# Program order and engine choice of the first feed-forward tiles rearranged in a fused linear-attention and feed-forward kernel

## The chip, the cores and the metric

The kernel runs on one core of a Trainium2 chip. The core has five engines with a queue each: TensorE (PE in the profile, its weight loads shown as PEld), VectorE (DVE), ScalarE (ACT), GpSimd (POOL) and SyncE (SP), which here issues every load and store. The metric is the device time of one execution in microseconds (us), taken as the median of several.

## The reference

For four batches and four heads, with 1088 positions of 32 numbers each, queries, keys and values go through a feature map: each vector x gives a = S1 x and b = S2 x (eight numbers each) and the 64 products a_i b_j. The output of the attention is

```
kv  = sum over positions of k_p[f] * v[d]        (64 x 32 for each batch and head)
z   = sum over positions of k_p[f]
num = q_p @ kv ;  den = q_p @ z + 1e-6 ;  x = num / den
```

The 4352 rows of x, 128 numbers wide (four heads of 32), then pass a feed-forward network with 2048 hidden units:

```
h = x @ w_in ;  r = max(h, 0) ;  g = s * r * r + b ;  out = g @ w_out
```

S1, S2, w_in and w_out arrive as 64-bit floats and are turned into 32-bit ones on the chip.

## The kernel before, in words

**Tiles.** The 4352 rows are cut into nine feed-forward tiles, number 0 with 256 rows and numbers 1 to 8 with 512. A tile has eight units (jp = 0 to 7), each 256 of the 2048 hidden units. A unit is a generator, `ffn(t, jp)`, named by two digits ("03" is tile 0, unit 3). Its steps are: the product into `hp` (PE, L571), the relu (L131 or L133), the square (L140 or L142), and the product into `ops` (PE, L571). In tile 0 the products use 32-bit operands directly, four matmul records for each product (two blocks of 128 hidden units, two records each). In tiles 1 to 8 each operand is split into a high and a low part of a faster type, `xh` and `xl`, `uh` and `ul`, `wih` and `wil`, `woh` and `wol`, and a product has six matmuls; `split_u` (L121 and L565) makes `uh` and `ul`.

**Weights.** w0 to w9 are ten weight blocks: even numbers are parts of w_in, odd ones of w_out; w0 to w3 have 256 columns, w4 to w9 have 512. `load_weights` (L185, steps "Lw0" to "Lw9") issues loads of 256 KB, one for a small block and two for a large one. `split_weights` (steps "w0" to "w9") turns a block into floats in three steps: a Prelu on ACT (L202, the "prelude" below), an integer scaling called bits (L127 on ACT or L125 on DVE), and a join on DVE (L193); then come the high part (L121) and the low part (L136). Raw blocks of w_in share four buffers, and so do those of w_out, so the fifth raw block of a kind waits on SP until the join of the first has read its buffer. The fifth of w_in is w4 in both orders; the loads of w_in before it are w0, w2, w8, w6 before the change and w2, w0, w8, w6 after it.

**Attention.** `first_keys` ("k0") makes the key features of batch 0 in three groups (PE L295, copies L121, outer products on DVE L136), `first_key_sums` ("e0", ended by `masked`, `spread` and `key_sums`) and `first_value_sums` ("v0", PE L253, 72 records) sum them; the constants and the values of batch 0 arrive in one load of 662 KB, `vc_sb` (L158). `kvphase` ("k1" to "k3") does the other batches. `direct_features` makes the query features of tiles 0 and 1 on the engines ("q0", "q1": PE L402, copies `br` L121, products `pq` on DVE L410), `stored_features` those of the others by way of DRAM ("q2" to "q8": PE L419, copy `abq`, stores L428, loads L435 and L439, a product). `first_denominators` ("d0"), `first_numerators` ("n0") and `attend` ("n1" to "n8") multiply features and sums (PE L464) and divide; n0 ends with `x` for tile 0 (DVE L495), and the first unit can start behind it.

**Order.** Nothing is scheduled by a machine at run time. `ORDER` is a list of steps; each token advances the generator of that name by one step, and each engine runs its instructions in the order in which the steps issued them. "Lk0" and its like are loads on SP's one queue, in order: a load that waits holds up all behind it. `ON_DVE` names the steps that run on DVE; those that are not named run on ACT (copies, relus, squares, bits) or on POOL (pairwise products). "c" and "z" are warming products of 256 and 512 columns (L650) whose result is never read. PSUM has two `hp` buffers, one `ops` and three `psa`.

```
for c in ORDER.split():
    next(gens[c], None)
```

The first ten loads before the change, in SP's order, are: the S matrices (80 KB), keys and queries of batch 0 (192 and 512 KB), w0, w2 (256 KB each), vc_sb (662 KB), the queries of tile 1, w8, w6 and w1 (256 KB each), 2,982 KB together. Then come w4, w6 (its second part), the queries of tile 2, w4 (second part), w3, w5, w5, w7, w7, w8 and the keys of batch 1. The first steps are the same work in the same place in both orders on PE: keys, q0, key sums, value sums, q1, turned sums, d0, n1, n0, q2 and then the units 00, 01, 03.

Of the kernel before, what the change touches and what calls it, by code (L numbers as in the profile page):

```python
# [38 lines left out]
DIRECT = (0, 1)  # L39
FIRST_F32 = (0, 1, 2, 3, 4, 5, 6, 7)  # L40
ORDER = """
c z Ls c z Lk0 c Lk0 Lw0 Lw2 s Lv0 Lq1 Lw8 z s c z c s s z z s w0 w2 k0 s c k0 Lw6 k0 k0 k0 Lw1 k0 k0 w0 k0 w0 Lw4
Lw6 q0 c q0 Lq2 k0 Lw4 q0 Lw3 Lw5 Lw5 Lw7 Lw7 e0 e0 q0 Lw8 Lk1 e0 v0 v0 q0 w2 Lk1 e0 v0 w2 v0 q1 q1 q1 q1 e0 e0 w1
v0 z w1 q1 d0 v0 n1 d0 n0 w6 w6 q2 d0 c w4 d0 d0 n0 n1 Lv1 w4 w4 w1 q2 w4 w3 00 00 00 01 w3 w0 03 01 01 w5 w6 q2 00
02 Lw9 03 w8 w3 n1 w3 n1 01 03 Lw9 02 w5 04 02 w7 q2 w5 w7 n1 Lk3 q2 w0 03 05 n1 05 Lk3 02 w8 Lq3 w1 05 Lq4 q1 n1 04
q2 n1 k1 w8 06 w6 w7 04 n1 w9 05 07 06 w3 04 k1 w4 06 k1 n1 w9 w9 k1 w9 07 13 k1 07 w1 Lv1 Lv3 w6 06 q2 w5 13 13 10
q2 07 q2 k1 k3 10 q3 10 q3 13 14 10 07 w2 q2 13 k1 k3 k1 12 w2 w5 14 q3 k1 10 15 w7 q2 07 12 Lv2 14 12 k1 q3 Lk2 k3
10 k3 12 Lv3 11 14 w8 k3 12 w7 n2 k3 15 12 14 w8 07 q3 w9 15 n2 n2 13 14 11 15 11 17 n2 n2 Lk2 15 n2 16 15 q3 q3 n2
n2 11 11 Lq6 17 q4 q3 k2 16 n2 n2 20 k3 16 11 16 17 q3 q4 25 16 q4 17 q3 k3 q4 q4 16 20 22 20 k2 17 17 25 25 20 25
17 20 22 17 24 20 q4 22 q3 k2 22 25 24 24 k3 q4 Lv2 23 22 n3 q4 Lq5 23 24 q6 n3 23 q6 22 n3 Lq8 n3 24 21 23 21 27 q6  # L50
21 n3 k2 q4 25 23 q6 21 n3 27 26 24 n3 23 k2 27 n3 21 k2 q6 27 q8 q6 n3 q6 q6 n3 26 q4 26 k2 21 q0 30 q8 q4 k2 k2 27
q6 26 33 q6 k3 30 k2 30 q8 26 q5 n4 q5 q8 33 32 n4 30 30 26 33 n4 27 n4 n4 33 n4 33 32 31 q6 32 34 n4 27 31 30 31 32
31 n6 32 Lq7 n4 31 q5 n6 35 q8 q8 n6 34 32 q5 n6 31 34 n6 n6 35 34 n6 35 q5 36 37 n6 n6 35 q8 34 n6 34 36 61 33 36
35 37 36 35 60 37 37 36 27 61 63 q5 36 37 q8 q5 37 q8 61 61 60 60 64 61 37 63 63 60 60 q8 64 n4 63 63 64 65 60 q5 62
q8 64 65 61 64 62 65 q7 n8 n4 63 62 67 q7 n8 65 65 n8 62 q5 n8 62 q7 n8 66 67 q5 67 64 66 67 q7 65 67 66 q5 66 40 n8
42 66 40 n8 40 42 62 41 42 n5 66 40 q7 n5 n5 67 40 n8 42 41 45 67 n5 q7 44 41 42 n5 q7 40 n5 n5 41 45 43 45 41 45 45
42 43 n5 45 44 43 44 43 47 46 41 44 43 47 47 44 67 43 q7 46 46 n8 n5 n5 47 46 47 51 51 54 q7 n8 51 44 46 50 54 54 q7
51 51 46 47 54 50 54 53 50 47 56 53 52 50 53 q7 50 n7 50 52 54 n7 52 53 47 55 53 51 52 55 n7 52 55 85 53 56 55 55 56
57 57 57 52 56 56 n7 n7 55 85 57 80 57 81 85 56 85 57 80 85 81 n7 80 81 80 57 80 83 83 81 84 80 85 86 81 83 83 83 81
84 84 82 84 86 84 86 n7 84 n7 n7 86 n7 87 82 82 83 57 86 87 71 87 72 87 82 82 72 87 72 71 86 72 70 72 71 82 70 74 71  # L60
87 71 70 70 76 70 74 87 70 37 73 76 76 74 76 71 72 74 76 73 75 74 77 73 76 73 73 75 87 75 73 77 75 77 74 75 75 77 77
77 77 77 77 77 77
"""
ON_DVE = frozenset("""
a4 a6 a7 e1 e2 e3 e4 e5 e6 e7 e8 k0 m2 m3 m4 m5 m6 m7 m8 o00 o03 o06 o10 o15 o20 o25 o30 o35 q40 q43 q44 q50
q52 q76 q80 q81 r22 r24 r33 r37 r50 r61 r63 r65 r66 r76 r77 r87 s0 sb t1 t2 u13 u16 u20 u24 u26 u32 u33 u34
u36 u41 u44 u45 u47 u51 u55 u56 u57 u60 u62 u63 u65 u70 u71 u72 u73 u77 u81 u82 u83 u86 w0h w0l w1h w1l w2h
w2l w3b w3h w3l w4b w4h w4l w5b w5l w6l w7l w8b w8l w9b w9h w9l x2 x3 x4 x5 x8 y0 y3
""".split())
NS = 32 * 2 + 2 * R  # L70
CS, CB, CT = 0, 1, 32
# [660 lines left out]
```

## Time and profile before

| | before |
|---|---|
| median of three runs | 230.12 us (229.19, 230.12, 230.51) |
| profiled execution | 230.27 us, span from first to last instruction 228.5 us |
| PE busy | 221.6 us, 97% of the span |
| PEld busy | 176.8 us, 77% |
| DVE busy | 189.1 us, 83% |
| ACT busy | 176.6 us, 77% |
| POOL busy | 4.4 us, 2% |
| bytes moved by DMA | 22.08 MB, of these 0.23 MB on queue q8, kind "instruction", in 14 packets |

Times in the views are in us from the first instruction of the span; the execution is 1.8 us longer than the span. Shares are averages over stages that differ: up to about 17 us the engines wait for each other and for loads, and after that PE has hardly a gap. A matmul's end is modelled, so that a busy PE may still lose time inside a run of matmuls.

### The profile page before, as it was taken

What the parts mean: (1) busy time and instruction counts of PE and PEld (TensorE: products, weight loads), DVE (VectorE), ACT (ScalarE), POOL (GpSimd) and SP (SyncE); (2) the same over time, 40 slices, a digit from 0 to 9 for tenths busy, and PEclk for the clock granted to TensorE, in tenths of its full rate; (3) what the DMA queues carried; (4) which work ended last, traced back from release to release, by engine and by line L of the source; (5) the groups of instructions that cost most, each with busy time, mean ns of one, the idle gap of its engine ahead of it and who ended that gap; (6) DMA issues with size and microseconds to landing.
All of it is one profiled execution on the core that took longest, in us unless ns stands there. A gap on an engine that the chain in (4) does not pass through costs nothing.

```text
span 228.5 us, 4620 instructions
## 1 busy us (share of the span) xinstructions
PE 221.6 (97%) x1839; PEld 176.8 (77%) x1839; DVE 189.1 (83%) x269; ACT 176.6 (77%) x211; POOL 4.4 (2%) x14
## 2 busy tenths in 40 slices
PE   8869999999999999999999999999999999999994
PEld 5648787787887877788887877888878888887883
DVE  1959899997889979999778988997976597968682
ACT  3469989997968969786965779669777969788671
POOL 1001130000000000000000000000000000000000
PEclk9999999999999999999999999999999999999999
DMA  6999582850147443044000220200100001001001
GB/s 206 369 363 342 170 268 94 268 147 5 46 141 218 136 138 109 25 156 147 0 0 5 92 68 35 82 0 0 46 3 1 0 24 68 0 3 46 0 0 46
DMA packets 12204, 22.08 MB, mean 97 GB/s; under 512 B 1304, under 2 KB 2840, under 8 KB 12184
## 3 DMA queue, kind: packets, MB, share of 16 engines
q1 hardware_dynamic: 12184, 21.80, 29.7%
q8 instruction: 14, 0.23, 0.4%
q14 instruction: 6, 0.05, 0.1%
HBM read 18.65 MB, written 3.15 MB: 95 GB/s over the span
## 4 chain that ended last, share of the span: by engine, by line
PE 93%; DMA 3%; SPq 1%; issue 1%; DVE 1%; ACT 1%
PE hp L571 42%; PE ops L571 42%; PE psa L464 4%; DMA vc_sb<-vc 3%; PE psa L253 2%; PE hp L419 1%; PE psa L352 1%; PE hp L402 0%; SPq L185 0%; SPq L158 0%; ACT ot L619 0%; DVE pq L410 0%; PE psa L274 0%; PE hp L464 0%; ACT br L121 0%
## 5 line engine op out<-in xcount | busy, mean ns | idle before, releaser
L565 DVE TENSOR_TENSOR ul<-u,uh 128x1024 fp32r<-128x1024 f32 x64 | 77.8, 1219 | 8.4 <-ACT uh L121 6.3
L133 ACT ACTIVATE u<-hp 128x1024 f32<-128x1024 f32 (+1 forms) x60 | 57.8, 966 | 20.7 <-PE hp L571 10.2
L142 ACT ACTIVATE u<-u 128x1024 f32<-128x1024 f32 (+1 forms) x64 | 64.1, 1006 | 4.9 <-DVE u L131 3.5
L571 PE MATMUL hp<-xh,wil 128*128 128x512 f32 x128 | 51.1, 399 | 0.0
L571 PE MATMUL ops<-uh,wol 128*128 128x512 f32 (+1 forms) x128 | 50.4, 394 | 0.0
L571 PE MATMUL hp<-xl,wih 128*128 128x512 f32 x128 | 49.9, 390 | 0.0
L571 PE MATMUL hp<-xh,wih 128*128 128x512 f32 x128 | 49.9, 390 | 0.0
L571 PE MATMUL ops<-uh,woh 128*128 128x512 f32 (+1 forms) x128 | 49.6, 388 | 0.0
L121 ACT CAST uh<-u 128x1024 fp32r<-128x1024 f32 x34 | 35.5, 1051 | 7.0 <-DVE u L140 3.4
L571 PE MATMUL ops<-ul,woh 128*128 128x512 f32 (+1 forms) x128 | 39.3, 388 | 0.0
L121 DVE CAST uh<-u 128x1024 fp32r<-128x1024 f32 x30 | 20.7, 690 | 11.1 <-ACT u L142 10.6
L571 PEld LDWEIGHTS ops<-uh,wol 128*128 128x128 f32 x128 | 24.0, 188 | 6.8 <-issue 1.6
L571 PEld LDWEIGHTS hp<-xh,wil 128*128 128x128 f32 x128 | 24.0, 188 | 6.2 <-ACT u L133 0.5
L571 PEld LDWEIGHTS hp<-xl,wih 128*128 128x128 f32 x128 | 24.0, 188 | 5.2
L571 PEld LDWEIGHTS ops<-ul,woh 128*128 128x128 f32 x128 | 23.9, 188 | 5.1
L571 PEld LDWEIGHTS ops<-uh,woh 128*128 128x128 f32 x128 | 24.0, 188 | 4.7
L571 PEld LDWEIGHTS hp<-xh,wih 128*128 128x128 f32 x128 | 24.1, 188 | 4.7
L131 DVE TENSOR_SCALAR u<-hp 128x1024 f32<-128x1024 f32 x12 | 14.7, 1224 | 1.9 <-PE hp L571 1.0
L464 PE MATMUL psa<-pq,st 64*32 64x256 f32 (+2 forms) x336 | 10.2, 330 | 1.0 <-issue 1.0
L136 DVE TENSOR_TENSOR ph<-kab 128x768 f32<-128x768 f32 (+2 forms) x9 | 10.8, 1214 | 0.1
L140 DVE TENSOR_TENSOR u<-u 128x1024 f32<-128x1024 f32 x8 | 9.6, 1214 | 0.4 <-ACT u L133 0.3
L202 ACT ACTIVATE w<-raw 128x512 f32<-128x512 f32 (+1 forms) x10 | 5.8, 583 | 4.6 <-DMA raw<-w_in 4.6
(86 smaller groups left out, 172.1 us busy)
## 6 DMA issues: line engine op xcount, KB each, us to landing
pq<-qd SPq DMA_DIRECT2D x14, 256.0 KB
br<-qd SPq DMA_DIRECT2D x28, 128.0 KB
raw<-w_in SPq DMA_DIRECT2D x8, 256.0 KB
qt<-qT SPq DMA_DIRECT2D x8, 256.0 KB
raw<-w_out SPq DMA_DIRECT2D x8, 256.0 KB
outT<-ot SPq DMA_DIRECT2D x7, 256.0 KB
kt<-kq SPq DMA_DIRECT2D x3, 320.0 KB
vt<-vc SPq DMA_DIRECT2D x3, 320.0 KB
```

The source lines that it names most:

```text
L121: (nc.vector.tensor_copy if key in ON_DVE else nc.scalar.copy)(out=out, in_=in_)
L131: nc.vector.tensor_scalar(out=out, in0=in_, scalar1=0.0, scalar2=None, op0=ALU.max)
L133: nc.scalar.activation(out=out, in_=in_, func=AF.Relu)
L136: (nc.vector if key in ON_DVE else nc.gpsimd).tensor_tensor(out=out, in0=in0, in1=in1, op=op)
L140: nc.vector.tensor_tensor(out=out, in0=in_, in1=in_, op=ALU.mult)
L142: nc.scalar.activation(out=out, in_=in_, func=AF.Square)
L202: nc.scalar.activation(out=out, in_=f32(high), func=AF.Prelu, scale=2.0 ** -112, alpha=2.0 ** 32)
L253: nc.tensor.matmul(out[32 * q:32 * q + 32], w, x, start=(q not in begun), stop=last, skip_group_check=True)
L352: nc.tensor.matmul(views[e][32 * q:32 * q + 32], sp[64 * e:64 * e + 64], kt[64 * e:64 * e + 64, a:a + w32], start=True, stop=True, skip_gr ...
L464: nc.tensor.matmul(out[r][32 * h:32 * h + 32, a:e], st_t[b][rows, y, h // 2, h % 2], x, start=(a == 0 and start), stop=True, skip_group_ch ...
L565: nc.vector.tensor_tensor(out=ul[:, :, :N], in0=u[:, :, :N], in1=f32(uh[:, :, :N]), op=ALU.subtract)
L571: nc.tensor.matmul(out, w, x, start=(first and k == 0), stop=(last and k == len(terms) - 1))
```

## The change

`ORDER` gets another sequence up to the first units of tile 4; its last 198 steps are the same. Every step of the work is still there once. There are four warming products more: c goes from 8 to 11, z from 7 to 8. w2 is loaded ahead of w0, w1 goes ahead of w8, and w8's second part and part of the keys of batch 1 go ahead of w7; q3's and q4's loads move forward. `ON_DVE` gains 22 names and loses 26. Names are made of a letter for the step and its number: q, r, u and two digits are square, relu and `uh` of a unit; wNb, wNh, wNl the bits, high and low part of a weight block; aN, xN, kN, tN copies of the attention; sb and s0 steps on the S matrices.

```
--- before.py
+++ after.py
@@ -39,33 +39,33 @@
 DIRECT = (0, 1)
 FIRST_F32 = (0, 1, 2, 3, 4, 5, 6, 7)
 ORDER = """
-c z Ls c z Lk0 c Lk0 Lw0 Lw2 s Lv0 Lq1 Lw8 z s c z c s s z z s w0 w2 k0 s c k0 Lw6 k0 k0 k0 Lw1 k0 k0 w0 k0 w0 Lw4
-Lw6 q0 c q0 Lq2 k0 Lw4 q0 Lw3 Lw5 Lw5 Lw7 Lw7 e0 e0 q0 Lw8 Lk1 e0 v0 v0 q0 w2 Lk1 e0 v0 w2 v0 q1 q1 q1 q1 e0 e0 w1
-v0 z w1 q1 d0 v0 n1 d0 n0 w6 w6 q2 d0 c w4 d0 d0 n0 n1 Lv1 w4 w4 w1 q2 w4 w3 00 00 00 01 w3 w0 03 01 01 w5 w6 q2 00
-02 Lw9 03 w8 w3 n1 w3 n1 01 03 Lw9 02 w5 04 02 w7 q2 w5 w7 n1 Lk3 q2 w0 03 05 n1 05 Lk3 02 w8 Lq3 w1 05 Lq4 q1 n1 04
-q2 n1 k1 w8 06 w6 w7 04 n1 w9 05 07 06 w3 04 k1 w4 06 k1 n1 w9 w9 k1 w9 07 13 k1 07 w1 Lv1 Lv3 w6 06 q2 w5 13 13 10
-q2 07 q2 k1 k3 10 q3 10 q3 13 14 10 07 w2 q2 13 k1 k3 k1 12 w2 w5 14 q3 k1 10 15 w7 q2 07 12 Lv2 14 12 k1 q3 Lk2 k3
-10 k3 12 Lv3 11 14 w8 k3 12 w7 n2 k3 15 12 14 w8 07 q3 w9 15 n2 n2 13 14 11 15 11 17 n2 n2 Lk2 15 n2 16 15 q3 q3 n2
-n2 11 11 Lq6 17 q4 q3 k2 16 n2 n2 20 k3 16 11 16 17 q3 q4 25 16 q4 17 q3 k3 q4 q4 16 20 22 20 k2 17 17 25 25 20 25
-17 20 22 17 24 20 q4 22 q3 k2 22 25 24 24 k3 q4 Lv2 23 22 n3 q4 Lq5 23 24 q6 n3 23 q6 22 n3 Lq8 n3 24 21 23 21 27 q6
-21 n3 k2 q4 25 23 q6 21 n3 27 26 24 n3 23 k2 27 n3 21 k2 q6 27 q8 q6 n3 q6 q6 n3 26 q4 26 k2 21 q0 30 q8 q4 k2 k2 27
-q6 26 33 q6 k3 30 k2 30 q8 26 q5 n4 q5 q8 33 32 n4 30 30 26 33 n4 27 n4 n4 33 n4 33 32 31 q6 32 34 n4 27 31 30 31 32
-31 n6 32 Lq7 n4 31 q5 n6 35 q8 q8 n6 34 32 q5 n6 31 34 n6 n6 35 34 n6 35 q5 36 37 n6 n6 35 q8 34 n6 34 36 61 33 36
-35 37 36 35 60 37 37 36 27 61 63 q5 36 37 q8 q5 37 q8 61 61 60 60 64 61 37 63 63 60 60 q8 64 n4 63 63 64 65 60 q5 62
-q8 64 65 61 64 62 65 q7 n8 n4 63 62 67 q7 n8 65 65 n8 62 q5 n8 62 q7 n8 66 67 q5 67 64 66 67 q7 65 67 66 q5 66 40 n8
-42 66 40 n8 40 42 62 41 42 n5 66 40 q7 n5 n5 67 40 n8 42 41 45 67 n5 q7 44 41 42 n5 q7 40 n5 n5 41 45 43 45 41 45 45
-42 43 n5 45 44 43 44 43 47 46 41 44 43 47 47 44 67 43 q7 46 46 n8 n5 n5 47 46 47 51 51 54 q7 n8 51 44 46 50 54 54 q7
-51 51 46 47 54 50 54 53 50 47 56 53 52 50 53 q7 50 n7 50 52 54 n7 52 53 47 55 53 51 52 55 n7 52 55 85 53 56 55 55 56
-57 57 57 52 56 56 n7 n7 55 85 57 80 57 81 85 56 85 57 80 85 81 n7 80 81 80 57 80 83 83 81 84 80 85 86 81 83 83 83 81
-84 84 82 84 86 84 86 n7 84 n7 n7 86 n7 87 82 82 83 57 86 87 71 87 72 87 82 82 72 87 72 71 86 72 70 72 71 82 70 74 71
-87 71 70 70 76 70 74 87 70 37 73 76 76 74 76 71 72 74 76 73 75 74 77 73 76 73 73 75 87 75 73 77 75 77 74 75 75 77 77
-77 77 77 77 77 77
+c z Ls s z c s z z Lk0 s c c Lk0 c Lw2 z z k0 c z k0 w2 Lw0 s s Lv0 k0 w2 k0 c w0 c z w0 Lq1 Lw1 Lw8 k0 c k0 w0 k0
+q0 Lw6 Lw4 Lw6 k0 k0 q0 Lq2 Lw4 q0 Lw3 q0 q0 e0 Lw5 e0 e0 w2 e0 v0 v0 v0 q1 w1 e0 v0 q1 Lw5 Lw8 Lk1 c q1 q1 Lw7 e0
+v0 d0 q1 v0 w0 w6 w1 s d0 n1 n0 w6 w4 d0 Lw7 q2 d0 d0 n0 n1 Lk1 w4 c q2 00 w3 w4 w1 00 01 w2 n1 w3 n1 w6 n1 00 w1 w3
+03 00 01 n1 w4 01 w5 q2 03 02 03 Lw9 Lq3 w5 w8 w5 n1 01 Lw9 04 03 Lq4 02 Lv1 02 w1 05 w4 n1 w8 02 w7 k1 05 w2 q2 w8
+05 w7 n1 04 04 w7 n1 Lk3 06 Lv1 05 04 k1 w6 q2 Lv2 q2 w9 Lk3 06 07 w9 k1 w8 06 w6 q2 Lk2 w0 w8 w9 q2 q2 q2 w5 13 06
+07 k1 07 13 w3 10 13 w7 k1 w5 07 10 k1 13 07 q3 k3 k1 w9 Lv3 k1 10 14 q3 Lv3 07 10 k3 13 w7 k1 07 k3 12 10 14 14 11
+k3 q3 12 q1 k3 q2 14 12 10 15 w3 12 14 k1 15 12 13 15 11 n2 n2 11 q3 12 n2 n2 n2 n2 Lk2 15 n2 11 15 14 11 17 16 15
+n2 17 17 k3 q4 w9 16 Lv2 k2 17 n2 q4 16 16 n2 20 17 q3 k2 q3 16 25 k2 16 20 20 k3 20 22 k3 20 25 25 24 q3 22 q4 q4
+11 q3 17 q3 22 q3 22 Lq6 k2 q3 17 n3 q6 22 n3 q6 n3 24 n3 20 25 23 21 q6 q6 24 25 24 23 25 24 27 24 n3 n3 q6 23 k2
+q4 q4 n3 23 21 21 23 21 26 Lq8 n3 26 Lq7 21 27 23 q6 q4 k3 q8 n3 q4 k2 22 n3 q4 26 q4 27 27 26 q4 k2 q8 30 27 Lq5 30
+21 k2 26 k2 33 30 k2 n4 q5 33 q6 32 26 k3 30 q8 n4 30 27 q6 33 n4 q5 q6 31 q6 33 32 n4 n4 27 q0 n4 n4 30 32 q6 33 n6
+n4 q5 q5 n6 q8 q8 34 32 n6 32 q8 31 31 31 31 35 q5 n6 q8 n6 31 q8 34 37 q5 32 n6 34 34 n6 35 35 35 27 34 37 36 33 q5
+n6 n4 35 36 34 n6 36 q5 n6 37 61 n4 35 36 q5 60 36 37 61 61 37 60 60 36 q8 q8 61 63 q8 61 64 60 63 37 37 65 60 60 63
+64 63 63 61 64 65 62 64 q7 n8 64 q7 65 65 63 17 62 62 n8 62 n8 65 n8 q7 67 67 64 67 66 q7 n8 q7 62 66 40 n8 67 67 66
+65 q5 n8 40 66 66 n8 q5 40 42 62 40 66 41 42 40 n5 42 42 67 41 41 42 45 n5 n5 n5 n5 67 41 q7 41 45 40 n5 45 43 44 n5
+n5 q7 45 45 42 43 45 44 43 44 43 47 46 41 44 43 47 47 44 67 43 q7 46 46 n8 n5 n5 47 46 47 51 51 54 q7 n8 51 44 46 50
+54 54 q7 51 51 46 47 54 50 54 53 50 47 56 53 52 50 53 q7 50 n7 50 52 54 n7 52 53 47 55 53 51 52 55 n7 52 55 85 53 56
+55 55 56 57 57 57 52 56 56 n7 n7 55 85 57 80 57 81 85 56 85 57 80 85 81 n7 80 81 80 57 80 83 83 81 84 80 85 86 81 83
+83 83 81 84 84 82 84 86 84 86 n7 84 n7 n7 86 n7 87 82 82 83 57 86 87 71 87 72 87 82 82 72 87 72 71 86 72 70 72 71 82
+70 74 71 87 71 70 70 76 70 74 87 70 37 73 76 76 74 76 71 72 74 76 73 75 74 77 73 76 73 73 75 87 75 73 77 75 77 74 75
+75 77 77 77 77 77 77 77 77
 """
 ON_DVE = frozenset("""
-a4 a6 a7 e1 e2 e3 e4 e5 e6 e7 e8 k0 m2 m3 m4 m5 m6 m7 m8 o00 o03 o06 o10 o15 o20 o25 o30 o35 q40 q43 q44 q50
-q52 q76 q80 q81 r22 r24 r33 r37 r50 r61 r63 r65 r66 r76 r77 r87 s0 sb t1 t2 u13 u16 u20 u24 u26 u32 u33 u34
-u36 u41 u44 u45 u47 u51 u55 u56 u57 u60 u62 u63 u65 u70 u71 u72 u73 u77 u81 u82 u83 u86 w0h w0l w1h w1l w2h
-w2l w3b w3h w3l w4b w4h w4l w5b w5l w6l w7l w8b w8l w9b w9h w9l x2 x3 x4 x5 x8 y0 y3
+a3 a6 a7 a8 e1 e2 e3 e4 e5 e6 e7 e8 k2 m2 m3 m4 m5 m6 m7 m8 o00 o03 o06 o10 o15 o20 o25 o30 o35 q24 q43 q44
+q50 q52 q63 q76 q80 q81 r27 r50 r65 r76 r77 r87 t2 t3 u13 u15 u17 u20 u23 u30 u34 u36 u37 u40 u41 u44 u45 u47
+u51 u55 u56 u57 u61 u62 u63 u65 u66 u67 u70 u71 u72 u73 u77 u81 u82 u83 u86 w0l w1h w1l w2h w2l w3b w3l w4b
+w4l w5b w5h w5l w6l w7b w7h w7l w8h w8l w9l x1 x2 x4 x5 x6 x8 y0 y3
 """.split())
 NS = 32 * 2 + 2 * R
 CS, CB, CT = 0, 1, 32
```

## Rows read from the trace of the kernel before

**Rows 1.** Busy time by stretch: stretch, length, engines, clock, DMA share, GB/s.

```profile
8.40:9.50 1.10, 0.02 (x4) 0.04 (x2) 1.10 (x3) 0.58 (x2) 0.09 (x1) 1.00 1.01 391
...
14.40:15.40 1.00, 0.00 (x0) 0.00 (x0) 0.70 (x3) 0.59 (x2) 0.00 (x0) 1.00 1.03 371
...
30.27:47.17 16.90, 16.90 (x332) 13.47 (x330) 15.95 (x24) 15.99 (x23) 1.36 (x1) 1.00 0.69 203
```

**Rows 2.** Chain of waits in order of time: start, length, what.

```profile
3.07 6.29 DMA vc_sb<-vc
...
9.49 1.21 PE psa L253 x72
...
12.41 0.70 DVE pq L410
...
14.39 1.01 issue
15.40 0.73 PE psa L464 x17
...
16.46 0.44 DVE x L495
...
16.94 2.95 PE hp L571 x12
```

**Rows 3.** DMA queues between 12.9 and 13.0 us: packets, MB, engine share.

```profile
q8 instruction: 1, 0.02, 69.5%
```

**Rows 4.** Waits of SP's queue: total, times, longest.

```profile
SPq L185 <- DVE w L193: 2.4, 1, 2.4
```

**Rows 5.** SP in order of time: start, length, line, operation.

```profile
4.99 0.57 SPq L185 DMA_DIRECT2D raw<-w_out  x1
8.74 0.80 SPq L185 DMA_DIRECT2D raw<-w_in  x2
...
10.06 0.43 SPq L185 DMA_DIRECT2D raw<-w_in  x1
```

**Rows 6.** DVE in order of time: start, length, what, idle before.

```profile
2.59 0.20 DVE L125 TENSOR_SCALAR s_bits<-s_raw 128x80 int32<-128x80 uint32 x1 [2.59 <-DMA s_raw<-s]
...
9.49 0.75 DVE L410 TENSOR_TENSOR pq<-hp,br 128x256 f32<-128x256 f32 x2
...
10.82 0.42 DVE L193 SCALAR_TENSOR_TENSOR w<-w,raw 128x256 int32<-128x256 int32 x1
...
14.72 0.45 DVE L475 STREAM_TRANSPOSE rr<-rc 128x256 f32<-128x256 f32 x1
```

**Rows 7.** ACT in order of time, columns as in rows 6.

```profile
6.33 0.44 ACT L202 ACTIVATE w<-raw 128x256 f32<-128x256 f32 x1 [2.91 <-DMA raw<-w_in]
...
13.25 0.46 ACT L127 ACTIVATE raw<-raw 128x256 int32<-128x256 uint32 x1
...
13.73 0.70 ACT L202 ACTIVATE w<-raw 128x512 f32<-128x512 f32 x1
14.31 0.68 ACT L127 ACTIVATE raw<-raw 128x512 int32<-128x512 uint32 x1
16.36 0.66 ACT L202 ACTIVATE w<-raw 128x512 f32<-128x512 f32 x1 [1.38 <-DMA raw<-w_in]
16.93 0.35 ACT L121 COPY abq<-hp 128x256 f32<-128x256 f32 x1
```

**Rows 8.** Costliest groups of the page: count, busy, mean ns, idle before.

```profile
L133 ACT ACTIVATE u<-hp 128x1024 f32<-128x1024 f32 (+1 forms) x60 | 57.8, 966 | 20.7 <-PE hp L571 10.2
...
L121 ACT CAST uh<-u 128x1024 fp32r<-128x1024 f32 x34 | 35.5, 1051 | 7.0 <-DVE u L140 3.4
...
L121 DVE CAST uh<-u 128x1024 fp32r<-128x1024 f32 x30 | 20.7, 690 | 11.1 <-ACT u L142 10.6
...
L131 DVE TENSOR_SCALAR u<-hp 128x1024 f32<-128x1024 f32 x12 | 14.7, 1224 | 1.9 <-PE hp L571 1.0
```

**Rows 9.** The warming products: ns shortest, median, longest; first and last start.

```profile
L650 PE MATMUL ops<-const-bfloat16-1.0 x15: 283/417/631, 0.8 to 16.6; 128*128 128x256 bf16 x8, 128*128 128x512 bf16 x7
```

## The prediction

> **What bounds the kernel now.** I read the page first: PE is busy 97% of the span, so a new order of the same work can gain only where PE waits or does work that nobody needs. Then the busy time by stretch [rows 1]: from 30.27 to 47.17 PE is busy for all of its 16.90 us, and so it is in every stretch from 16.94 to the last product. Before that there are holes: 1.08 of 1.10 us from 8.40 to 9.50, and the whole microsecond from 14.40 to 15.40. The granted clock reads 1.00, the 2.4 GHz level, in the stretches of both holes and after them, so a hole costs its own length and no slower clock behind it.
>
> The chain of waits [rows 2] says what the holes are. The first ends when the load of the constants and values of batch 0 lands at 9.36 (3.07 + 6.29): a load bounds it. The second, "issue", 14.39 to 15.40, lies inside one run of small products of `attend` for tile 1 (x17 more records follow it on the same line): PE waited for nothing that a semaphore tells. Behind it come n0's products, x at 16.46 and the first unit at 16.94. The DMA view of a short stretch [rows 3] shows one instruction packet that begins between 12.9 and 13.0; 69.5% of 16 engines over 0.1 us is 1.11 us on one DMA engine, so it ends near 14.05, 1.35 before PE goes on. I read the hole as PE waiting for its program. No row names PE as that packet's owner, nor when it was asked for; both are inference.
>
> Why so late? The DMA engines are full: share 1.01 and 391 GB/s in the first hole, 1.03 in the second [rows 1]. A weight load issued at 10.06 has its last reader waiting until 16.36, 6.3 us later [rows 5, 7]. Whatever joins the DMA engines near 9.5 stands behind all loads issued until then.
>
> Once the units run, PE sets the end, but DVE and ACT have little to spare: 15.95 and 15.99 of 16.90 us between 30.27 and 47.17 [rows 1].
>
> **The change part by part.**
>
> *Loads.* SP's first ten loads are the same set; w2 and w0 change places and so do w8, w6 and w1, which leaves the bytes ahead of the load that lands at 9.36 equal. The eleventh (w4, fifth raw block of w_in) waits for a join. Today it is w0's, and SP issues it at 8.74 after 2.4 us of waiting, the queue having stopped at 5.56 (4.99 + 0.57) [rows 4, 5]. In the new order it is w2's, which stands on DVE behind the second `pq` of q0. That product ends at 10.24 today [rows 6]; ACT's new order (w2 ahead of the first copies) can push it back by up to 0.3, so the join of 0.42 ends between 10.7 and 11.0; I take 10.95. All on SP behind it goes 2.2 us later (10.95 - 8.74): w6's second part, tile 2's queries, w4's second part, w3, w5, w8, the keys of batch 1, w7. ACT's preludes wait for these, and through ACT's queue the copy of q2 and the relus.
>
> What does that delay cost? At 9.36 the ten loads have 1,024 KB left; at 391 GB/s they last 2.6 us, to 12.0. The DMA engines are still busy when w4 joins them, or just run dry. A load into an empty queue lands at most 2.59 us after its issue (the first one, counted from the span's start [rows 6]). So w4 lands by 13.5, and at 0.67 us for each 256 KB the next three follow at 14.2, 14.9 and 15.6: w4 is whole by 15.6, against 16.36 now. The bounds are 15.0 (no gap in the stream) and 18.6 (the 2.2 us passed on in full); I take 15.6, because [rows 1] show throughput, not issue, as the limit.
>
> *The program fetch.* With SP silent from 5.56 to 10.95, a packet asked for near 9.5 has only the ten loads ahead, done by 12.0. Then 1.11 us of transfer and the same 1.35 until PE moves: 14.46 at the latest, where PE needs it at 14.39. The hole of 1.01 goes to between 0 and 0.1. The steps ahead of it keep their places on PE: value sums at 9.49, q1, then d0, which waits today for the first `pq` of q1, done at 13.11 (12.41 + 0.70) [rows 2], as in the new order. So n1 runs through, n0 follows, and x's products are ready at 16.46 - 1.01 = 15.45. What is late next: the reciprocals, ready at 15.17 (14.72 + 0.45) [rows 6], 0.28 earlier. The first unit starts at 16.94 - 1.01 = 15.93. **Gain 1.01.**
>
> *ACT's queue behind it.* New order: w6's prelude, w1's bits, w6's bits, w4's prelude, the copy of q2, w3's prelude, the first relu. w6 is whole at 14.2: prelude 0.70, bits 0.46 and 0.68 end at 16.0; w4's prelude 0.66 ends at 16.7 and the copy 0.35 at 17.05 [rows 7]. The second unit's product wants its `hp` buffer, which that copy frees, at 15.93 + 0.98 = 16.91 (12 records in 2.95 are three products [rows 2]). **Given back 0 to 0.2; I take 0.1.**
>
> *Four more warming products.* At the median of 417 ns [rows 9] 1.7 us; between the key products they push these back, but the value sums can't start before 9.36, and PE stands idle for 1.08 now; shortest times (283) give 1.1. Cost nothing; without the cover 1.1 to 1.7. The c behind q1 lies where PE waits for `pq`, the one ahead of the first unit where PE waits for x.
>
> *The S matrices on ACT.* Two small steps move from DVE to ACT, some 0.2 us later; PE is still in its first eleven warming products. The copies into `srep` now stand behind w2's prelude, which can't start before 6.33 [rows 7], and q0 has moved behind all key products. Cost nothing, because v0 waits for the load; without that, up to 0.9 (two more small steps behind 6.33 + 0.44).
>
> *Engines of units.* Of the feed-forward steps 9 `uh` go to DVE and 6 come back, 1 relu goes and 7 come back. At the means of [rows 8] DVE gets 3 x 0.69 - 6 x 1.22 = -5.2 us, ACT -3 x 1.05 + 6 x 0.97 = +2.7. Off the path: PE is full there. It matters as slack: units that start 1.0 earlier use up what [rows 1] leave (0.95 on DVE, 0.91 on ACT in 16.90), so up to 0.5 may come back as short waits; that is in the range.
>
> *Later moves on PE and SP* (k3's sums some units later, n3 earlier, q3, q4 and k2's loads): same products, needed microseconds after their loads; nothing.
>
> **Sum.** 230.27 (the profiled execution) - 1.01 + 0.1 = 229.36. That execution is 0.15 above the median of 230.12; on the median's basis 229.2.
>
> **The rivals.**
>
> *The hole stays.* The Trainium skill (Runtime: NRT & Kernel Launch, "Instruction fetch mechanics") says that an engine's program comes in 16 KiB blocks fetched while the present one runs, at a cost that is "mostly hidden". It also says (DMA: Bandwidth & Descriptors, "Queues, rings and completion order") that a DMA engine alternates between its rings at packets, so that a fetch would not stand behind the loads. By these the hole is no fetch, or one that fewer loads don't hasten. As a mechanism of this kernel: PE stops again after about as many instructions, x is as late as now, and the time stays at 230.1. For it: the 1.35 us between packet and restart, which I can't explain. Against it: the packet and the hole are the only ones of their kind in the first 17 us, and no semaphore ended the wait. 9%.
>
> *ACT takes the wait over.* w6's prelude heads ACT's queue; should w6 land 0.9 later than I have it, at 15.1, the copy of q2 ends near 17.95, where the second product starts today (16.94 + 0.98 = 17.92), and all of the gain is gone: 230.1. For it: nothing on ACT can overtake. Against: the throughput above. 8%.
>
> *Slower: the loads land late in full.* If the 2.2 us at SP pass on whole, w4 is there at 18.6, its prelude starts 0.57 before the copy, which ends 18.6 + 0.57 + 0.35 = 19.5, and the second product starts 1.6 later than now; w3 and w5 follow in the same stream. 231.8. It decides from a landing of w4 at 17.0; over 0.5% needs 18.1. For it: SP's silence, with w3, w5, w7, w8 behind it. Against: the engines have 12.0 - 9.36 of work left when the silence ends. 13%.
>
> *More than the hole.* Shifted slots and better balanced engines also take 0.3 to 0.6 us of short waits inside the run of units: 228.7. For it: 5.2 us less on DVE. Against: PE shows no gaps there. 10%.
>
> **How the numbers follow.** A measurement of this kernel can tell about 0.5%, 1.15 us: below 228.97 is faster, above 231.27 slower. The forecast has 60%, with its own range 228.7 (no loss behind the hole and some small waits gone) to 229.8 (0.5 given back to DVE and ACT); some 23 points of it lie under 228.97. With the last rival faster has 0.33. Same: 37 of the forecast, 9 and 8 of the two first rivals, 0.54. Slower 0.13. The range 228.5 to 230.5 holds the forecast, the two rivals at 230.1 and the better half of the gaining one, and leaves out the slower one.
>
> **What would show it.** Right: no "issue" of 1 us in PE's chain before the first unit; x's product near 15.5 and the first unit at 15.9; an instruction packet that begins before 12.0; SP's eleventh load near 10.95; w4's prelude before 16.4; every stretch after 17 full of PE. Wrong: a hole of about 1 us inside n1 or n0 with the packet after 12.9; a first unit at 15.9 but a second product that waits on ACT past 17.5; w4's prelude ended by a DMA at 17 or later; PE gaps at 30 to 55 ended by DVE's `ul` or ACT's relus.

## The result, and the profile after

The changed kernel takes 233.33 us in the median of five runs (233.02, 238.48, 235.35, 232.89, 233.33), the kernel before 230.12 on the same chip. The ratio is 1.0126, 95% interval 1.0081 to 1.017, so the change is slower by more than the 0.5% that can be told; 229.2 had been predicted, with a range of 228.5 to 230.5. The runs of 238.48, which the ratio leaves out, and 235.35 had a mean granted clock of 0.986 and 0.985, the other three 1.00. The profiled execution is the one of 233.02 us, span 231.1.

First the start, where the gain was forecast. Chain of waits of the changed kernel, from q0 on (to set beside [rows 2]):

```profile
13.54 1.15 PE psa L464 x28
...
15.28 0.44 DVE x L495
...
15.76 1.48 PE hp L571 x5
```

n1's products run without a gap (28 of its 32 records are one piece of the chain), x comes at 15.28 and the first unit at 15.76, against 16.94. Up to here the new kernel leads by 1.18, a little more than predicted. Further on in the same chain:

```profile
33.61 1.32 PE psa L253 x87
34.93 0.37 PE hp L419 x13
35.30 0.90 issue
...
37.08 1.12 PE hp L571 x4
...
77.69 0.57 SPq L439
...
78.36 5.23 DMA qt<-qT
...
83.70 1.22 DVE pq L136
...
87.06 0.21 DVE kvs L121
...
87.31 0.49 PE psa L274 x2
...
90.97 0.42 PE hp L571
```

The same places in the chain of the kernel before:

```profile
34.77 1.32 PE psa L253 x87
...
36.95 2.94 PE hp L571 x12
...
88.31 1.60 PE hp L571 x6
```

Read side by side they give the balance. At k1's sums (L253) the lead is 1.16. From there to the next unit the new kernel takes 3.47 (33.61 to 37.08), the old one 2.18; 0.90 of it is a stop named "issue" between two of q3's small products, and the lead is gone (37.08 against 36.95). At 88.31 and 90.97 both stand behind the same steps, and the new one is 2.66 late; it stays so to the end (spans 231.1 and 228.5). What lies between is one chain: the last load of q4 is issued at 77.69, q4's product on DVE (`pq`, L136) starts at 83.70, and PE goes on at 87.31. The waits of PE in the changed kernel name the two places (engine, line, what ended the wait; total, times, longest):

```profile
PE psa L274 <- DVE kvs L121: 2.3, 1, 2.3
PE hp L419 <- issue: 0.9, 1, 0.9
```

Why does PE wait for `kvs`, a copy of 0.28 us? DVE in order of time in the changed kernel, with the idle time before an instruction and what ended it in brackets:

```profile
83.70 1.22 DVE L136 TENSOR_TENSOR pq<-pq,br 128x1024 f32<-128x1024 f32 x1 [3.86 <-DMA qt<-qT]
84.85 0.18 DVE L266 TENSOR_TENSOR zh<-psa,vc_sb 128x32 f32<-128x32 f32 x1
...
86.98 0.28 DVE L121 COPY kvs<-psa 128x128 f32<-128x128 f32 x1
```

and the kernel before, DVE and one row of ACT:

```profile
81.78 0.19 DVE L266 TENSOR_TENSOR zh<-psa,vc_sb 128x32 f32<-128x32 f32 x1 [1.46 <-PE psa L253]
...
82.69 1.23 DVE L136 TENSOR_TENSOR pq<-pq,br 128x1024 f32<-128x1024 f32 x1 [0.15 <-DMA br<-qd]
```

```profile
82.44 0.27 ACT L121 COPY kvs<-psa 128x128 f32<-128x128 f32 x1
```

The product starts at nearly the same time in both, 82.69 and 83.70: when its loads have landed (the view names tile 5's `qt` as the releaser, the load issued right behind them; the product itself reads `pq` and `br`). But before, it stood behind the masked sums of batch 2 (`masked`, L266), and `kvs` was ACT's. In the new order the product stands ahead of the masked sums, and `k2` is one of the names that `ON_DVE` gained, so both steps that PE's turned sums (L274) need are queued behind a product that waits 3.86 us for a load.

On SP, the eleventh load was issued right behind w0's join (SP, to set beside [rows 5], then DVE):

```profile
8.88 0.33 SPq L185 DMA_DIRECT2D raw<-w_in  x1
```

```profile
8.43 0.42 DVE L193 SCALAR_TENSOR_TENSOR w<-w,raw 128x256 int32<-128x256 int32 x1
```

and ACT began with w4 earlier, at 15.79 against 16.36 (to set beside [rows 7]):

```profile
15.79 0.66 ACT L202 ACTIVATE w<-raw 128x512 f32<-128x512 f32 x1
16.35 0.34 ACT L121 COPY abq<-hp 128x256 f32<-128x256 f32 x1
```

### The profile page after: what moved, and what is told of

Its sections match the earlier page's. It is cut to its first block, busy times and chain, and to the rows that moved or that the text cites. A ratio compares the mean times of both kernels' runs of the same rounds, so it can differ in the third digit from the quotient of the medians.

```text
span 231.1 us, 4612 instructions
## 1 busy us (share of the span) xinstructions
PE 221.9 (96%) x1843; PEld 176.7 (76%) x1843; DVE 185.7 (80%) x265; ACT 178.6 (77%) x215; POOL 3.2 (1%) x14
## 4 chain that ended last, share of the span: by engine, by line
PE 87%; DMA 5%; SPq 3%; DVE 2%; issue 1%; ACT 1%; DVEq 0%
PE hp L571 40%; PE ops L571 38%; PE psa L464 4%; DMA vc_sb<-vc 3%; DMA qt<-qT 2%; PE psa L253 2%; SPq L439 1%; PE hp L419 1%; PE psa L352 1%; SPq L435 1%; DVE pq L136 1%; DVE ul L565 0%; ACT br L121 0%; PE hp L402 0%; SPq L176 0%
## 5 line engine op out<-in xcount | busy, mean ns | idle before, releaser
L133 ACT ACTIVATE u<-hp 128x1024 f32<-128x1024 f32 (+1 forms) x66 | 64.0, 969 | 23.5 <-DVE ul L565 11.8
L142 ACT ACTIVATE u<-u 128x1024 f32<-128x1024 f32 (+1 forms) x63 | 63.2, 1007 | 3.1 <-DVE u L131 1.6
L121 ACT CAST uh<-u 128x1024 fp32r<-128x1024 f32 x31 | 32.5, 1052 | 8.5 <-PE ops L571 4.3
L121 DVE CAST uh<-u 128x1024 fp32r<-128x1024 f32 x33 | 22.7, 688 | 10.8 <-ACT u L142 9.8
L136 DVE TENSOR_TENSOR pq<-pq,br 128x1024 f32<-128x1024 f32 x7 | 8.5, 1218 | 3.9 <-DMA qt<-qT 3.9
L140 DVE TENSOR_TENSOR u<-u 128x1024 f32<-128x1024 f32 x9 | 10.9, 1215 | 0.1
L136 DVE TENSOR_TENSOR ph<-kab 128x768 f32<-128x768 f32 (+2 forms) x9 | 10.8, 1212 | 0.1
L511 DVE STREAM_TRANSPOSE dt<-psa 128x256 f32<-128x256 f32 x16 | 6.8, 437 | 4.5 <-PE psa L464 4.4
```

The lines of the kernel that those rows point to most:

```text
L121: (nc.vector.tensor_copy if key in ON_DVE else nc.scalar.copy)(out=out, in_=in_)
L133: nc.scalar.activation(out=out, in_=in_, func=AF.Relu)
L136: (nc.vector if key in ON_DVE else nc.gpsimd).tensor_tensor(out=out, in0=in0, in1=in1, op=op)
L140: nc.vector.tensor_tensor(out=out, in0=in_, in1=in_, op=ALU.mult)
L142: nc.scalar.activation(out=out, in_=in_, func=AF.Square)
L511: nc.vector.transpose(out=dt[:, r * M:(r + 1) * M], in_=den[r])
```

## The experiments

Each ratio is to the kernel before on the same chip. The edits are moves in `ORDER`, shown by their surroundings; each step is still there once.

**q4's six reading loads ahead of q6's stores on SP.**

```
-25 23 21 q6 q6 24 25 ... 23 k2 q4 q4 n3 ... 23 q6 q4 k3 q8 n3 q4 k2 22 n3 q4 26 q4 27
+25 23 21 q4 q4 q4 q4 q4 q4 q6 q6 24 25 ... 23 k2 n3 ... 23 q6 k3 q8 n3 k2 22 n3 26 27
```

> The changed kernel (233.0 us in its profile), with the six reading loads of tile 4's query features (two pq, four br) put ahead of tile 6's stores on SP. Load theory: the changed order made SP wait for tile 6's copy (to 68.2 us) and its stores before it could read tile 4's features back, though these had been stored by 57.7; the product of tile 4 on DVE then waited until 83.7 and held up batch 2's masked sums and their copy behind it, for which PE stood 2.3 us. With the loads ahead of the stores the product starts right behind n3's xl (79.8), PE has no wait of over 0.3 us at the turned sums of batch 2, and the profile is at 230.4 us (233.0 less 2.6). Rival, DVE too full: the wait comes from the work on DVE before these sums, whatever the loads do; then PE still waits 1.5 us or more there and the time stays at 232 to 233.

229.69 (median of ten), ratio 0.9958 [0.9921, 0.9996]: the loss is gone, and the wait at L274 with it. Its profiled execution took 234.14, for another reason (chain of waits, then busy time by stretch as in [rows 1]):

```profile
14.22 0.56 issue
...
35.73 0.36 PE hp L419 x13
36.10 2.31 issue
```

```profile
39.60:43.00 3.40, 3.40 (x12) 2.82 (x11) 3.40 (x6) 1.09 (x2) 0.00 (x0) 0.50 0.45 150
```

The "issue" stops stand in n1, as in the kernel before, and in q3, as in the changed one, here 0.56 and 2.31 long. As they delay PE, the trace of both moves below shows the missing wait more plainly. From 1.2 us behind the longer one the granted clock is at 0.50, the 1.2 GHz level, for 3.4 us.

**q4's product alone later on DVE**, behind k2's `kvs`; loads as in the change.

```
-26 q4 27 27 26 q4 k2 q8 30 27 Lq5 30 21 k2 26
+26 q4 27 27 26 k2 q8 30 27 Lq5 30 21 k2 q4 26
```

> The changed kernel, with one step moved: tile 4's product on DVE goes behind batch 2's masked sums and copy (no load moves). Load theory with its second half, that only DVE's fixed order carried the late load to PE: the load still lands near 83.6, but PE's wait of 2.3 us at the turned sums goes, and the product is done before n4 needs it (about 86.5); 230.5 to 231.0 us. Rival, the late load itself is what counts: the wait moves on to n4's products and the time stays at 232.5 to 233.

230.59 (ten), ratio 0.9991 [0.9942, 1.0041]. DVE in order of time:

```profile
79.72 0.19 DVE L266 TENSOR_TENSOR zh<-psa,vc_sb 128x32 f32<-128x32 f32 x1 [1.10 <-PE psa L253]
...
81.86 0.29 DVE L121 COPY kvs<-psa 128x128 f32<-128x128 f32 x1
82.77 1.23 DVE L136 TENSOR_TENSOR pq<-pq,br 128x1024 f32<-128x1024 f32 x1 [0.62 <-DMA qt<-qT]
```

The product is as late as ever (82.77), and nobody waits for it. So the loss is the product's place, with the load's lateness as its size: mending either one removes it.

**q2's four `br` loads later**, off the stretch ahead of the stop in q3.

```
-w6 q2 Lk2 w0 w8 w9 q2 q2 q2 w5 ... q3 Lv3 07 10
+w6 Lk2 w0 w8 w9 w5 ... q3 Lv3 q2 q2 q2 q2 07 10
```

> The changed kernel, with tile 2's four br loads (27.9 to 30.9 us on SP) put behind the values of batch 3, which SP can't issue before 35.0. Fetch theory: the hole of 0.9 us on PE at 35.3, inside tile 3's small products, is PE waiting for its program, whose packet began at 33.43 behind those loads; with the DMA engines idle by then the packet begins 1 us earlier or more, the hole is 0.2 or less, and the time falls by 0.9 to 1.2 us to about 232.0. Rival: the hole is no program wait, and stays between 0.7 and 1.0 at the same place; 233.0.

232.49 (four), ratio 1.0116 [1.0032, 1.0199]. The stop at q3 is gone from its profile, and nothing is won (waits of PE):

```profile
PE psa L274 <- DVE kvs L121: 2.9, 1, 2.9
```

q4's product still starts at 83.34 (83.70 in the change); what PE wins ahead of it, it waits longer there.

**Both moves of loads.**

> Both moves of loads at once: tile 4's reading loads ahead of tile 6's stores, tile 2's br loads behind the values of batch 3. If both theories hold, what the changed order won before the first unit (1.18 us: the unit starts at 15.76 against 16.94) is no longer given back, and the profile is at 229.1 us, 1.1 under the kernel before. Rival: DVE and ACT, near full in tiles 1 to 3, give most of it back in short waits; 229.8 to 230.3 us.

229.51 (229.03 to 230.12, ten), ratio 0.9952 [0.9922, 0.9982], profiled execution 229.12. Busy time by stretch:

```profile
30.00:46.00 16.00, 16.00 (x243) 12.38 (x242) 14.20 (x20) 13.16 (x20) 0.00 (x0) 1.00 0.49 158
70.00:92.00 22.00, 22.00 (x257) 17.97 (x256) 19.13 (x31) 17.47 (x21) 0.00 (x0) 1.00 0.32 97
```

PE is full in both stretches, as it was in the third row of [rows 1]. By the two ratios this version is 1.7% faster than the change, and 0.5% faster than the kernel before, at the edge of what can be told.

**The kernel before once more**, to see whether its stop of 1.01 us belongs to the kernel or to one execution.

> The kernel before, unchanged, for a second trace of it. Fetch theory: how late the program packet is differs from execution to execution; if the packet begins again near 12.9 us the hole of 1.0 us stands again behind the 15th record of n1, if it begins before about 12.0 there is no hole or a shorter one and the first unit starts at 15.7 to 16.3 instead of 16.94; either way a hole can only stand at that one record. Rival: the hole is a wait of the program's own, and is the same 1.0 us whenever the packet comes.

229.39, span 227.6. Chain of waits:

```profile
13.60 0.68 PE psa L464 x15
14.28 0.00 issue
14.28 0.73 PE psa L464 x17
...
15.82 1.35 PE hp L571 x5
```

No stop: the split at the same record (x15, then x17) is 0.00 long, and the first unit starts at 15.82, 0.06 behind the changed kernel's. The instruction packet began at 11.93 here and between 12.9 and 13.0 in [rows 3].

**The kernel before with ten small products ahead of q0**, which count as 20 more PE records: if the stops hang on the count of instructions, each comes 20 records earlier in the work.

```
-k0 w0 Lw4 Lw6 q0 c q0 Lq2
+k0 w0 Lw4 Lw6 y y y y y y y y y y q0 c q0 Lq2
```

> The kernel before, with ten warming products of 32x32 put ahead of q0 (two matmul records and two weight loads each, 40 instructions of PE, run while it would wait for the constants). Fetch theory: a program packet is used up after a fixed number of PE's instructions, so that the hole moves 20 matmul records up the program, from behind n1's 15th record into d0 (behind its 11th or 12th), and since the packet is asked for about 1.5 us earlier it is shorter, 0 to 0.6; the time falls by 0 to 0.8 us. Rival: the hole belongs to n1 (a wait on a buffer or a copy) and stays behind the 15th record of n1; the time is that of the kernel before.

230.68 (ten), ratio 1.002 [0.9975, 1.0065]. The time is that of the kernel before. The first packet came at 10.9 and left no stop, neither in d0 nor in n1; a later one did, in k1's sums (chain of waits):

```profile
33.61 1.32 PE psa L253 x82
34.93 2.16 issue
37.09 0.30 PE psa L253 x3
```

Counted over PE's product records, 470 stand ahead of the stop in q3 in the changed kernel and in the version with q4's loads first, and 469 here (a record or two may be missing), though the work there is another. In n1 it is 221 in the kernel before and in that version. Counted over all of PE's records, weight loads and semaphore instructions too, it is 449 ahead of each stop in n1 and 961 ahead of each stop in q3, and 960 here, where one product record is missing (1859 weight loads, 1858 products). These stops follow the first and the third packet of queue q8, two packets and 512 records apart: by this count a packet carries 256 of PE's records. That ties the packets to PE, which the prediction could only infer.

**The engines of before under the order of the "both" version.**

> Both moves of loads, and the engine choices put back to those of the kernel before; order and loads of the changed kernel otherwise. Theory of the prediction: engines of single steps are off the path while PE is full, at most 0.5 us, so 229.3 to 230.0. Rival: the start is 1.2 us earlier only because the new choices let DVE and ACT keep up; with the old ones PE waits 1 us or more for them between 16 and 60 us; 230.5 or more.

246.14 (four), ratio 1.0736 [1.0659, 1.0814]. Waits of PE:

```profile
PE ops L571 <- ACT ot L638: 3.2, 1, 3.2
PE psa L274 <- ACT kvs L121: 1.9, 1, 1.9
PE hp L571 <- DVE u L131: 1.8, 1, 1.8
```

The 48 names that change engine are units, weight steps and attention copies together, and the run doesn't tell them apart. A part of the loss is clock: it is at 0.50 from 91.0 to 94.4 and from 155.9 to 159.2 us. With `kvs` back on ACT, PE still waits 1.9 for it, behind a relu there.

**The engines of after under the order of before**, the mirror.

> The order before the change, with the engine choice of the change (the mirror of the run that put the old engine choice under the new order and gave 1.07). Theory A, engine choice and order are one schedule: the queues of VectorE and ScalarE are in order, so the old order with the new engines loses too, at least 5 us (ratio over 1.02), with waits of TensorE on both. Theory B, the engine choice of the change is simply the better one: the ratio is within 0.995 to 1.005 of before. The loss in the one run would then come from single choices that the old set has wrong, in any order.

238.82 (three), ratio 1.0366 [1.0264, 1.0469]:

```profile
PE hp L571 <- ACT u L133: 2.7, 6, 0.9
...
PE psa L274 <- DVE kvs L121: 0.5, 1, 0.5
```

Both mixtures lose. Neither list of engines is the better one by itself; each fits its own order, since DVE and ACT take their steps strictly in turn.

**The "both" version without its four added warming products** (three c, one z).

> Both moves of loads, without four warming products (one of 512 columns, three of 256) between the key products of batch 0. Theory of the prediction: they cost nothing, as the value sums wait for their load; 229.5 as with both moves alone (within 0.3), and the program's boundary falls 8 instructions later. Rival: they keep the granted clock up when loads come late; without them single executions lose 1 us or more and the median rises to 230 or more.

229.57 (ten), ratio 1.0012 [0.9973, 1.0052], no different from before's, as that of the version with them (0.9952) hardly is; the two intervals overlap. But four of the ten took 231.19 to 231.81, as the rival had it of single executions, where the version with them had none over 230.12. The two were run on different chips, the four have mean clocks of 0.997 to 1.00, and none has a profile: whether the warming products matter stays open.

**The changed kernel once more.**

> The changed kernel again, one look. Theory A, the loss is a fixed late load of tile 4's queries and a program packet whose time varies: the wait of TensorE at the turned sums of batch 2 stands again, 2.0 to 3.2 us near 85 us, whatever the start and the hole at q3 do; the hole at q3's 13th record is there or not, with a packet that begins at another time than 33.43. Theory B, both are marks of that one execution: the wait at the turned sums is under 1 us or gone, and the span is under 229.

232.35, span 230.4: PE's longest wait and the chain at q3:

```profile
PE psa L274 <- DVE kvs L121: 3.0, 1, 3.0
```

```profile
34.75 0.45 PE hp L419 x15
35.20 0.59 PE psa L352 x10
```

The stop at q3 is absent (from k1's sums to the next unit it takes 2.36, not 3.47) and the wait for q4's product is there again, longer by what the rest won. Set beside the kernel before's second execution (span 227.6, no stop either), the difference of 2.8 us is this wait (3.0), with some 0.2 won ahead of it.

## Why the prediction was wrong, step by step

**The step that failed** is "Later moves on PE and SP ... same products, needed microseconds after their loads; nothing". It weighed the moves on PE and SP and left out DVE, where q4's product had been put ahead of k2's masked sums. The term should have been +2.3 to +3.0 us. The waits in three traces were that long (2.3, 2.9 and 3.0). The material was in the trace of before (SP):

```profile
76.78 3.09 SPq L439 DMA_DIRECT2D br<-qd  x5
```

The third of these five is q4's last load, issued at 78.06, and its product starts at 82.69, right behind a masked sum that PE needs soon. What stands behind a waiting step was asked of the first 17 us alone. Moving the product alone, or the loads alone, takes the loss away. Nor had the engines of the attention copies, `k2` among them, and of the weight steps any term in the sum.

**The hole of 1.01** went, as predicted, and more than its size was won in that trace (1.18). The mechanism named, PE waiting for a program packet, fits: at five stops in four executions PE went on 1.34 to 1.69 us after the packet's end, and the stops follow the count of records. But as a gain of the change it was mis-sized: the kernel before loses this hole by itself in another execution, whose first unit (15.82) is 0.06 to 0.23 behind those of the changed kernel's two (15.76 and 15.59), and with the new start a stop of 0.56 stood at the same count in the version with q4's loads first. Against an execution without the hole the term is worth 0.06 to 0.23. The sum took one execution's accident for a property of the kernel. That loads decide how late the packet is isn't shown: with q2's loads moved, three profiled executions have the packet at 32.24, 32.24 and 32.53 and no stop in q3; with them in place, four have it at 32.30 and 32.46 without a stop and at 33.43 and 35.66 with one.

The Trainium skill (Runtime: NRT & Kernel Launch, "Instruction fetch mechanics") calls the cost of block crossings mostly hidden. The traces agree for most of the 14 packets of an execution; the rest cost 0.56 to 2.31 us here.

**SP's eleventh load** was forecast for 10.95, behind w2's join. It was issued at 8.88, right behind w0's join (8.43 + 0.42 on DVE): w4 can't have waited for w2's join, which starts at 10.31; it took the buffer of w0, though w2 had been loaded first, so the fifth block does not always wait for the first. SP was silent from 5.83 to 8.88, much as before (5.56 to 8.74), so the rival of late loads had nothing to stand on; and the earlier packet, 11.61, owes nothing to it.

**ACT's queue** gave nothing back: w4's prelude at 15.79, ahead of the 16.4 that was set as its test, and the copy of q2 over at 16.69. **Warming products and the S matrices** cost nothing that the start shows; the run without the products leaves it open whether they matter later.

**"Engines of units ... off the path", at most 0.5**, doesn't hold for the lists as a whole: with the other order's list the kernel loses 3.7 to 7.4%, and among PE's waits there are units' relus (2.7 us in one run, 1.8 in the other). How much the units alone make wasn't run. In the change itself they cost nothing that shows: with both moves of loads PE is full in the two stretches above. The busy sums moved as worked out in sign (DVE 189.1 to 185.7, ACT 176.6 to 178.6); sums of busy time don't tell what an in-order queue does.

## What to carry to other kernels

When steps move in queues that run in order, go through every engine's list and ask of each step that waits for a load what now stands behind it and who needs that; a step that nobody needs soon belongs behind one that PE needs next. Look at a second execution before a single stall is counted as a gain, above all one that no semaphore explains. Removing a wait ahead of a fixed late arrival wins nothing until the arrival is mended.

## What the runs showed of the hardware

The program packet for the same place came at other times in each execution: in the kernel before at 12.94 and 11.93, in the changed one at 33.43 and 32.30. The stop it leaves was 0 to 2.31 us long; the five that were longer than 0 stood at one of two counts of PE's records, 449 and 961.

In or behind a stop the clock can fall. Behind the stop of 2.31 us it fell 1.2 us after PE had gone on. In the version with q2's loads later it fell within the wait: PE stood from 84.03 to 86.95, and the granted clock was at 0.50 from 86.0 to 92.8 (PE, then busy time by stretch):

```profile
86.95 0.80 PE L274 MATMUL psa<-vc_sb,kvs 128*128 128x128 f32 x2 [2.92 <-DVE kvs L121]
```

```profile
86.00:92.80 6.80, 5.85 (x71) 4.72 (x74) 3.19 (x6) 4.26 (x6) 0.00 (x0) 0.50 0.23 67
```

In the changed kernel's two profiled executions the waits of 2.3 and 3.0 us, and in the version with ten small products the stop of 2.16, were followed by no such fall (mean clock 1.00), so the length of the stop alone doesn't decide.
